# Soft-capped attention followed by mixture-of-experts attention on one core: joined score fills, gates and slot sums on GpSimd, and a different order of the work

## The chip, the cores and the metric

The kernel runs on one core of a Trainium2 chip. The metric is device microseconds (us) of one execution; the kernel before took a median of 336.59 us over 3 runs (334.86 to 338.03). The engines are TensorE (PE, with its weight loads as PEld), VectorE (DVE), ScalarE (ACT), GpSimd (POOL) and SyncE (SP, which here only issues transfers). Each runs its own instructions in the order in which they were written, and waits on semaphores for the others.

## What is computed

Two stages. The first is attention with a soft cap over 8 batches, 12 heads, 448 positions and a head width of 64; the second is a mixture of four attention experts on its output.

```python
# stage 1, for each of B=8 batches and H=12 heads; S=448, Dh=64, cap=30
scores = cap * tanh((q @ k.T / sqrt(64)) / cap)
attn = softmax(scores)                   # over the keys
x = attn @ v                             # heads side by side: 8 x 448 x 768
# stage 2, E=4 experts, the two best of each position
logits = x @ w_gate                      # 768 -> 4
topk = the two largest logits;  w = softmax over these two
for e in range(4):
    a = softmax(causal(x @ wq[e] @ (x @ wk[e]).T / sqrt(64)))
    ye = a @ (x @ wv[e]) @ wo[e]         # 64 -> 768
    out += (e in topk) * w_of_e * ye     # 8 x 448 x 768, float32
```

## The kernel before

**Pairs and batches.** The first stage goes by pairs of heads: 6 pairs in each of 8 batches, 48 in all (`NP`, with `HP` = 6). In a matmul a pair takes the two halves of the 128 rows, 64 for each head. One pair is made up as follows, with the lines of the code in brackets.

- SP issues loads of q, k and v (float32) for two pairs at a time. The last 64 of the 448 keys, the tail, are loaded apart. GpSimd casts all of it to float16 (k L485, q L488, k tails `ktz` L493, v L497, v tails `vtz` L504); of pairs 0 and 1, VectorE casts k, q and the k tails.
- PE transposes q and k (L513, L523) into one PSUM bank, and VectorE copies it to the tile `qk` (L544; L534 for pair 0).
- PE makes the scores (function `fill`). X is a PSUM tile of 3 banks, Y one of 2. X takes key block 0 of both heads, as two matmuls over 64 rows each (L555), and the tail keys of both heads, as one matmul over all 128 rows (L564, called sT). Y takes key block 1 (Y1), and once it has been read, key block 2 (Y2); each is two 64-row matmuls at L555. A matmul over 64 of the rows is called half-row below, one over all of them full-row.
- ACT takes the tanh of X, Y1 and Y2 (L577) into the tile `yp`, and then one exp over the 7 x 448 columns of the pair (L587). In order of time ACT does, for each pair, tanh X, tanh Y1, the exp of the pair before, tanh Y2.
- PE multiplies by v (L600 tails, L607), with a column of ones beside v that gives the row sums. VectorE divides (L627, L629). PE transposes the result (L641), and VectorE copies it to `xT` (L649), which is x of the batch, transposed.

**The gate stage.** When the 6 pairs of a batch are done, the second stage of this batch is mixed into the pairs of the next one. It works with two slots, one for the best expert of a position and one for the second best.

- PE computes v of all experts and the four logits (L662); VectorE copies the logits to `lg` and the values to `vB` (L671, L674). PE computes q and k of the experts (L686).
- The gate: VectorE compares all pairs of logits of a position (`g_c`, `g_d`, L711 to L715), sums the comparisons to a rank (L717), makes a mask for each slot by comparing with the tiles `rank0` and `rank1` (`ms`, L720), and finds the difference of the two best logits with two maxima (L722 to L726). ACT takes one small exp of it (`gexp`, L731). VectorE turns that into the weights `mw` (L739 to L745).
- GpSimd spreads the masks over 64 columns (`mB`, L753), PE transposes them (L763), and VectorE multiplies q with them (`qm`, L771). So the scores of a slot are those of the chosen expert.
- PE makes the scores of a slot in the banks of X (L792), ACT takes the exp (L801), GpSimd cuts the causal triangle. PE multiplies by `vB` (L850) and VectorE divides and weights (`oB`, one for each slot, L863 and L865).
- PE transposes the sum of the two slots: L880 multiplies both with the identity and accumulates, 16 matmuls in a batch. VectorE copies to `oT` (L888), PE multiplies by wo (L903), VectorE copies to `ob` (L912), and SP stores it.

The gate stage of batch 7 has no pairs beside it. Function `last` does it with more parallel work (L945, L954, L966, L987 to L1094).

**The order.** The order on each engine comes from a planner in the kernel's own Python (`Graph`). Each step is an `Op` with an engine, a duration `occ`, a time `lat` after which its result can be used, and what it reads and writes. ACT's main steps (tanh, exps) are a fixed chain that sets due times (`dues`); `solve` then walks in time, and takes for each engine the ready step with the earliest due time, by these numbers. Steps whose name is in `first` (fills, transposes of q and k, their casts and copies) go ahead of others. Steps that need a PSUM bank take one of A0 to A2; some may also borrow banks of X when they would give it back in time. The planner works with estimated durations, and the program it leaves is fixed.

**The start.** Seven matmuls of zeros (L1122) run on PE before the first data come. Loads of the expert weights (L455) and memsets (L393, for instance) stand on GpSimd's queue among the first casts.

## Time and profile before

| | before |
|---|---|
| median of 3 runs | 336.59 us |
| the profiled execution: its own time | 336.45 us |
| its span | 334.4 us |
| PE busy | 293.5 us (88%), 3435 instructions |
| ACT busy | 291.7 us (87%), 232 instructions |
| DVE busy | 239.2 us (72%), 752 instructions |
| POOL busy | 160.6 us (48%), 451 instructions |
| mean granted clock of TensorE | 0.99 |

The span is the time from the first to the last instruction of the profiled execution; its own time includes what lies around that. In rows that begin with a time, the columns are the start in us, the duration in us (of all, where several follow each other and a count such as x4 stands at the end), the engine, the line, the operation, what it writes <- what it reads, and in brackets the idle time just before it and what ended that. In rows of waits the columns are the line that waits <- the line that released it, then the sum in us, the number of waits, and the longest. In rows that begin with a line, the sum in us and the mean in ns stand behind the first bar, the engine's idle time before them behind the second.

### The profile page before, as it was taken

What the parts mean: (1) busy time and instruction counts of PE and PEld (TensorE: products, weight loads), DVE (VectorE), ACT (ScalarE), POOL (GpSimd) and SP (SyncE); (2) the same over time, 40 slices, a digit from 0 to 9 for tenths busy, and PEclk for the clock granted to TensorE, in tenths of its full rate; (3) what the DMA queues carried; (4) which work ended last, traced back from release to release, by engine and by line L of the source; (5) the groups of instructions that cost most, each with busy time, mean ns of one, the idle gap of its engine ahead of it and who ended that gap; (6) DMA issues with size and microseconds to landing.
All of it is one profiled execution on the core that took longest, in us unless ns stands there. A gap on an engine that the chain in (4) does not pass through costs nothing.

```text
span 334.4 us, 8992 instructions
## 1 busy us (share of the span) xinstructions
PE 293.5 (88%) x3435; PEld 193.5 (58%) x3435; DVE 239.2 (72%) x752; ACT 291.7 (87%) x232; POOL 160.6 (48%) x451
## 2 busy tenths in 40 slices
PE   6777779998998989998999899998998899978873
PEld 2244456475656756575666756675656666655542
DVE  5133536876859788877898778877896788756683
ACT  2699999989999899999989999999998999699152
POOL 8689889866216752376243941476243501110030
PEclk9998989999999999999999999999999999999999
DMA  9999999978923647338624845430211002200224
GB/s 162 228 262 236 254 237 224 254 173 229 266 91 126 193 114 234 102 85 226 156 105 119 225 129 186 128 104 2 98 47 25 3 15 81 74 0 2 96 71 167
DMA packets 65291, 46.21 MB, mean 138 GB/s; under 512 B 25888, under 2 KB 61856, under 8 KB 65248
## 3 DMA queue, kind: packets, MB, share of 16 engines
q1 hardware_dynamic: 54032, 43.30, 47.9%
q0 software_dynamic: 10512, 1.58, 7.2%
q10 hardware_dynamic: 704, 0.75, 0.8%
q8 instruction: 27, 0.44, 0.6%
q14 instruction: 16, 0.13, 0.1%
HBM read 36.19 MB, written 11.01 MB: 141 GB/s over the span
## 4 chain that ended last, share of the span: by engine, by line
PE 56%; DVE 17%; POOL 7%; DMA 6%; issue 5%; ACT 5%; SPq 1%; ACTq 0%; DVEq 0%; POOLq 0%
PE A L607 7%; PE A L686 7%; PE A L662 6%; PE Y L555 5%; PE A L903 5%; PE A L600 4%; DVE oB L865 3%; PE A L641 3%; DMA ktf<-in_k_dram 3%; PE X L792 3%; PE X L564 3%; PE A L850 2%; ACT yp L577 2%; PE X L555 2%; DVE oT L888 2%
## 5 line engine op out<-in xcount | busy, mean ns | idle before, releaser
L587 ACT ACTIVATE yp<-yp 128x3136 f16<-128x3136 f16 (+2 forms) x49 | 135.7, 2772 | 0.0
L577 ACT ACTIVATE yp<-Y 128x896 f16<-128x896 f32 x96 | 88.8, 925 | 10.0 <-PE Y L555 9.2
L577 ACT ACTIVATE yp<-X 128x1344 f16<-128x1344 f32 x48 | 62.5, 1302 | 3.7 <-PE X L555 2.2
L607 PE MATMUL A<-v,yp 128*128 128x65 f16 x1152 | 58.1, 197 | 0.0
L607 PEld LDWEIGHTS <-yp 128*128 128x128 f16 x1152 | 51.7, 100 | 4.6 <-issue 3.0
L497 POOL CAST v<-vf 128x384 f16<-128x384 f32 x48 | 24.5, 509 | 54.4 <-issue 36.2
L600 PE MATMUL A<-vtz,yp 128*128 128x130 f16 x192 | 43.2, 226 | 6.6 <-ACT yp L587 3.0
L629 DVE TENSOR_TENSOR xk<-A,rca 128x256 f16<-128x256 f32 x96 | 40.5, 423 | 2.7
L485 POOL CAST k<-kf 128x384 f16<-128x384 f32 x46 | 23.3, 506 | 30.8 <-PE A L523 18.9
L544 DVE COPY qk<-A 128x960 f16<-128x960 f16 x47 | 29.6, 650 | 11.7 <-PE A L513 11.4
L627 DVE RECIPROCAL rca<-A 128x4 f32<-128x4 f32 x96 | 16.9, 177 | 28.0 <-PE A L607 27.6
L555 PE MATMUL Y<-qk 64*128 64x448 f16 x192 | 36.2, 373 | 0.7 <-ACT yp L577 0.5
L912 DVE COPY ob<-A 128x384 f32<-128x384 f32 (+1 forms) x55 | 29.3, 552 | 3.2 <-PE A L903 2.4
L488 POOL CAST q<-qf 112x512 f16<-112x512 f32 x46 | 28.3, 615 | 2.8 <-DMA qf<-in_q_dram 1.6
L903 PE MATMUL A<-wo,oT 128*128 128x384 f16 x114 | 26.6, 328 | 1.8 <-DVE oT L888 1.3
L600 PEld LDWEIGHTS <-yp 128*128 128x128 f16 x192 | 18.9, 99 | 15.2 <-issue 9.3
L753 POOL CAST mB<-ms 128x1024 f16<-128x1024 f32 x14 | 14.2, 1041 | 27.2 <-DVE ms L720 25.8
L555 PEld LDWEIGHTS <-qk 64*128 64x128 f16 x288 | 14.2, 93 | 22.0 <-issue 16.9
L523 PE MATMUL A<-ident,k 128*128 128x128 f16 x144 | 16.9, 229 | 10.5 <-POOL k L485 7.1
L504 POOL CAST vtz<-vtf 64x64 f16<-64x64 f32 x96 | 22.7, 236 | 3.1
L513 PE MATMUL A<-ident,q 112*128 112x112 f16 x192 | 23.1, 223 | 1.2 <-POOL q L488 1.2
L493 POOL CAST ktz<-ktf 64x64 f16<-64x64 f32 x92 | 21.6, 235 | 3.6 <-DMA ktf<-in_k_dram 0.3
(140 smaller groups left out, 569.2 us busy)
## 6 DMA issues: line engine op xcount, KB each, us to landing
qf<-in_q_dram SPq DMA_DIRECT2D x23, 448.0 KB, 6.4
kf<-in_k_dram SPq DMA_DIRECT2D x23, 384.0 KB, 5.3
vf<-in_v_dram SPq DMA_DIRECT2D x23, 384.0 KB, 5.1
out_dram<-ob SPq DMA_DIRECT2D x23, 384.0 KB, 2.9
out_dram<-ob SPq DMA_DIRECT2D x8, 192.0 KB, 2.7
ktf<-in_k_dram SPq DMA_DIRECT2D x46, 32.0 KB, 5.0
vtf<-in_v_dram SPq DMA_DIRECT2D x46, 32.0 KB, 4.7
qf<-in_q_dram ACTq DMA_DIRECT2D x2, 224.0 KB, 4.0
```

What stands on the lines that cost most here:

```text
L488: put(0.4, 0.56, lambda e: e.tensor_copy(q16[i], qf[s][:, h].rearrange("p h (c d) -> p c h d", c=QC)), [("qf", x)], [("q16", i)], head, f" ...
L497: nc.gpsimd.tensor_copy(v16[u][:, :, :, 0:Dh], vf[s][:, h].rearrange("p h (c d) -> p h c d", c=KC))
L544: lambda: nc.vector.tensor_copy(qk[t], bank16(g)[:, 0 : S + 512]),
L555: nc.tensor.matmul(dst[:, g, 0:S], qk[t][r, S + 128 * (c + 1) : S + 128 * (c + 2)], qk[t][r, 0:S], start=True, stop=True,)
L577: ACTS[what, p] = act(c_act(S * (b - a)), lambda: nc.scalar.activation(y[:, a:b, :], src[:, 0 : b - a, 0:S], AF.Tanh, scale=isc / capf), [ ...
L587: act(c_act(S * (b - a), False), lambda a=a, b=b: nc.scalar.activation(y[:, a:b, :], y[:, a:b, :], AF.Exp, scale=capf), ks, ks, fixed=True ...
L600: nc.tensor.matmul(ps[:, n, :, :], y[:, 2, w : w + 128], vtz[u], start=(n == 0), stop=False, skip_group_check=True,)
L607: nc.tensor.matmul(ps[:, n, h, :], y[:, SLOT[c][h], w : w + 128], v16[u][:, h, c, :], start=False, stop=(c == 2), skip_group_check=True,)
L629: dve(c_dve(256), lambda g=g, i=i, rc=rc: nc.vector.tensor_tensor(xk[p % NXK][:, 2 * i : 2 * i + 2, :, :], view(g)[:, :, :, 0:Dh], rc.broa ...
L686: pe(S, lambda g=g, w2=w2, j=j: nc.tensor.matmul(bank(g)[:, 0:S], w2[:, j, :], xT[x][:, j, :], start=(j == 0), stop=(j == NDC - 1)), [("xT ...
L903: nc.tensor.matmul(bank(g)[:, 0 : D // 2], oT[x][r][:, w : w + 128], wo2[r][:, c0:c1], start=(r == 0), stop=(r == 1),)
L912: e(o[lo:128, c0:c1], bank(g)[lo:128, 0 : D // 2])
```

## The change

It has five parts.

1. **Joined fills.** `fill` makes the Y2 scores of a pair and the X scores of the next pair one step of four half-row matmuls, where no gate-stage score stands between them (33 of 47 places). Counted from 0, the two slots of a batch are scored beside pairs 5 and 6 after it where it was 4 and 5 (`XOFF`), those of batch 6 beside 4 and 5 where it was 3 and 4.
2. **The gate on GpSimd.** All of it before the small exp, and the weights `mw` after it, are GpSimd operations. The form is another one: a signed difference, sums by halves (`g_h`, `g_k`) and constants in place of the rank tiles. Two operations after the exp stay on VectorE.
3. **Slot sums on GpSimd.** Two GpSimd additions make `oS`, the sum of the slots, in float16; PE transposes it with 8 transposes in a batch where 16 accumulating matmuls stood.
4. **The start.** Zero matmuls: 9 of 512 columns, then 30 of 128 columns wherever PE has nothing else (`NWARM`, `NFILL`). Pair 0's k cast is ACT's, the q casts of pairs 0 to 3 are VectorE's, all k tails are GpSimd's. Casts and transposes of each pair are written one pair earlier. The expert weights' loads are due 12 us later.
5. **The planner's numbers.** A change between half-row and full-row work costs 0.1 (`SWITCH`); PE takes twice as long before 5.5 us (`WARM`); transfers share a wire (`LAND`, `RATE`); due times follow the lag of ACT's chain; one solve stands where three did, each of which started from the times of the one before.

```diff
+SWITCH = 0.1
+WARM = 5.5
+LAND = 2.9
+NWARM = 9
+NFILL = 30
+RATE = 230.0
...
+            if e == "PE" and o.half != half:
+                t = max(t, free.get(e, 0.0) + SWITCH)
...
-                    d = u.due if u.first else max(u.due, t0 + 0.8)
-                    return d - (u.grp is not None and not u.opens), u.due, u.idx
+                    d = u.due + lag if u.first else max(u.due + lag, t0 + 0.8)
+                    d -= u.grp is not None and not u.opens
+                    return d - 2.0 * (u.half and half), u.due, u.idx
...
+        if p == 0:
+            act(c_act(KM, False), lambda: kc(nc.scalar.copy), *kio, name=f"k16_{p}", fixed=True)
+        else:
+            gp(0.45, lambda: kc(nc.gpsimd.tensor_copy), *kio, name=f"k16_{p}")
+        if p < 4:
+            dve(0.48, lambda: qc(nc.vector.tensor_copy), *qio, name=f"q16_{p}", lat=0.56)
+        else:
+            gp(0.56, lambda: qc(nc.gpsimd.tensor_copy), *qio, name=f"q16_{p}")
...
+        if what == "X" and p and p - 1 not in exps:
+            pass
+        elif what == "Y2" and p < NP - 1 and p not in exps:
+            pe(0, lambda: (heads(p, "Y2"), heads(p + 1, "X")), rd(p) + rd(p + 1),
+               both + [("s", XB[0]), ("s", XB[1])], occ=0.385, name=f"sY2X_{p}",
+               takes=YB + XB[0:2])
+        else:
+            pe(0, lambda: heads(p, what), rd(p), both, occ=0.195, name=f"s{what}_{p}",
+               takes=bs[0:2])
...
-        V = nc.vector
+        V = nc.gpsimd
...
+        g_(lambda: V.tensor_tensor(g_c[x], lb(), la(), ALU.subtract), L, ["c"], 0.22)
+        g_(lambda: V.tensor_scalar(g_d[x], g_c[x], 0.0, None, ALU.is_equal), [(b, "c")], ["d"],
+           0.2)
...
+        for i in range(2):
+            n = slice(2 * i, 2 * i + 2)
+            gp(1.1, lambda n=n: nc.gpsimd.tensor_tensor(oS[:, n], oB[0][:, n], oB[1][:, n], ALU.add),
+               [("oB", s, m) for s in range(2) for m in (2 * i, 2 * i + 1)], [("oS", i)],
+               name=f"oS{b}")
...
+                for n in range(4):
+                    nc.tensor.transpose(
+                        bank16(g)[:, 128 * n : 128 * (n + 1)],
+                        oS[:, n, 2 * r : 2 * r + 2, :].rearrange("p e d -> p (e d)"),
+                        ident if n < 3 else swap,
+                    )
...
-    XOFF = (4, 5)
...
+    XOFF = (5, 6)
+    exps = {HP * (b + 1) + (XOFF if b < LB - 1 else (4, 5))[s]: (b, s) for b in range(LB) for s in range(2)}
...
+    for i in range(NWARM + NFILL):
+        n = 512 if i < NWARM else 128
...
-    for _ in range(3):
-        G.dues(when)
-        order = G.solve(AUX, XB + YB)
-        when = {o.idx: o.start for o in fixed}
+    G.dues(when)
+    order = G.solve(when, AUX, XB + YB)
```

Some rows of the order show it at three places. The names end in the number of a buffer; lines are those of the kernel that the rows come from, so that a fill is L555 before and L580 now, and sT is L564 before and L601 now.

On PE, at the second Y fill of pair 3, before (`qk3` is the q and k of pair 3, `qk0` here that of pair 4, and `xk1` is a finished result that is being transposed; the two half-row matmuls that fill X from `qk0` stand ahead of its four transposes, the last of which is the first row):

```order
L641 MATMUL A1_66<-pswap_183,xk1_125 128x128
L564 LDWEIGHTS qk0_116
L564 MATMUL X_63<-qk0_116 128x448
L555 LDWEIGHTS qk3_119
L555 MATMUL Y_64<-qk3_119 128x448
L555 LDWEIGHTS qk3_119
L555 MATMUL Y_64<-qk3_119 128x448
L523 LDWEIGHTS k16_0_91
```

And now, at the same fill:

```order
L601 LDWEIGHTS qk0_116
L601 MATMUL X_63<-qk0_116 128x448
L580 LDWEIGHTS qk3_119
L580 MATMUL Y_64<-qk3_119 128x448
L580 LDWEIGHTS qk3_119
L580 MATMUL Y_64<-qk3_119 128x448
L580 LDWEIGHTS qk0_116
L580 MATMUL X_63<-qk0_116 128x448
L580 LDWEIGHTS qk0_116
L580 MATMUL X_63<-qk0_116 128x448
L681 LDWEIGHTS xk1_125
```

The half-row matmuls of X, which stood ahead of the transposes of `xk1` and of sT, now stand directly behind those of Y; of the four changes between half-row and full-row work, two are left.

The start: on VectorE before, the casts of pairs 0 and 1 (`q16`, `k16`, and the tails `ktz`) and the copy to `qk0`:

```order
L488 CAST q16_0_88<-qf0_68 112x512
L485 CAST k16_0_91<-kf0_72 128x384
L493 CAST ktz0_94<-ktf0_80 64x64
L488 CAST q16_1_89<-qf0_68 112x512
L493 CAST ktz0_94<-ktf0_80 64x64
L485 CAST k16_1_92<-kf0_72 128x384
L534 COPY qk0_116<-A1_66 128x576
L493 CAST ktz1_95<-ktf0_80 64x64 x2
```

On GpSimd now, behind the memsets, with `wvg` the weights for v and the gate:

```order
L419 MEMSET ktz5_99 128x128
L476 DMA wvg_181<-in_moe_w_gate_dram 128x6x4
L476 DMA wvg_181<-in_moe_wv_dram 128x6x64
L515 CAST ktz0_94<-ktf0_80 64x64
L476 DMA wvg_181<-in_moe_wv_dram 128x6x64
L515 CAST ktz0_94<-ktf0_80 64x64
L476 DMA wvg_181<-in_moe_wv_dram 128x6x64
L498 CAST k16_1_92<-kf0_72 128x384
L515 CAST ktz1_95<-ktf0_80 64x64 x2
```

The tails of pairs 0 and 1 went from VectorE to GpSimd, where issues of the weights' loads stand ahead of them and between them.

The gate of batch 1: on VectorE before, its first operations (`lg1` the logits, `qB1` and `kB1` the experts' q and k):

```order
L671 COPY lg1_137<-A2_67 128x4
L674 CAST vB1_135<-A2_67 64x4x64
L712 TENSOR_TENSOR g_d1_192<-lg1_137 128x64
L711 TENSOR_TENSOR g_c1_190<-lg1_137 128x64
L713 TENSOR_TENSOR g_d1_192<-g_d1_192,tri_186 128x64
L722 TENSOR_REDUCE g_m11_198<-lg1_137 128x4
L715 TENSOR_TENSOR g_c1_190<-g_c1_190,g_d1_192 128x64
L694 CAST qB1_1_141<-A1_66 128x448
L649 COPY xT0_132<-A0_65 128x448
L627 RECIPROCAL rca2_130<-A2_67 128x4
L717 TENSOR_REDUCE g_r1_194<-g_c1_190 128x16
```

On GpSimd now, from the slot sums of the batch before:

```order
L929 TENSOR_TENSOR oS_158<-oB0_156,oB1_157 128x512 x2
L753 TENSOR_TENSOR g_c1_189<-lg1_137 128x64
L754 TENSOR_SCALAR g_d1_191<-g_c1_189 128x64
L756 TENSOR_SCALAR g_c1_189<-g_c1_189 128x64
L757 TENSOR_TENSOR g_d1_191<-g_d1_191,tri_187 128x64
L758 TENSOR_TENSOR g_c1_189<-g_c1_189,g_d1_191 128x64
L760 TENSOR_TENSOR g_h1_197<-g_c1_189 128x32
L762 TENSOR_TENSOR g_r1_193<-g_h1_197 128x16
L766 TENSOR_SCALAR ms01_205<-g_r1_193 128x16
L766 TENSOR_SCALAR ms11_207<-g_r1_193 128x16
L807 CAST mB0_146<-ms01_205 128x1024
L807 CAST mB1_147<-ms11_207 128x1024
```

The gate left VectorE's queue, where copies of other steps stood between its operations, and stands on GpSimd's in one piece, with both mask casts right behind it and ahead of the four operations that give the small exp its input.

## What was predicted before the kernel ran

> **What bounds the kernel now.** I read the page first, for the span and the busy shares.
>
> ```profile
> span 334.4 us, 8992 instructions
> PE 293.5 (88%) x3435; PEld 193.5 (58%) x3435; DVE 239.2 (72%) x752; ACT 291.7 (87%) x232; POOL 160.6 (48%) x451
> ```
>
> Two engines are close to full: TensorE (PE) at 88% and ScalarE (ACT) at 87%. VectorE (DVE) has a quarter free and GpSimd (POOL) half. The profiled execution took 336.45 us, so 2.05 us lie outside its span; the median of the runs, 336.59, is 0.14 above it, and I count from 336.45. Next, ACT in order of time: the first work, one pair in the steady state, and the end of the softmax stream.
>
> ```profile
> 8.52 0.92 ACT L577 ACTIVATE yp<-Y 128x896 f16<-128x896 f32 x1 [1.75 <-PE Y L555]
> 12.07 1.29 ACT L577 ACTIVATE yp<-X 128x1344 f16<-128x1344 f32 x1 [0.59 <-PE X L564]
> 15.36 0.92 ACT L577 ACTIVATE yp<-Y 128x896 f16<-128x896 f32 x1 [2.00 <-PE Y L555]
> 21.80 0.92 ACT L577 ACTIVATE yp<-Y 128x896 f16<-128x896 f32 x1 [0.83 <-PE Y L555]
> ...
> 25.32 0.91 ACT L577 ACTIVATE yp<-Y 128x896 f16<-128x896 f32 x1
> 26.12 1.29 ACT L577 ACTIVATE yp<-X 128x1344 f16<-128x1344 f32 x1
> 27.29 0.93 ACT L577 ACTIVATE yp<-Y 128x896 f16<-128x896 f32 x1
> 28.09 2.84 ACT L587 ACTIVATE yp<-yp 128x3136 f16<-128x3136 f16 x1
> 30.79 0.94 ACT L577 ACTIVATE yp<-Y 128x896 f16<-128x896 f32 x1
> ...
> 299.11 1.03 ACT L801 ACTIVATE pB<-X 128x1024 f16<-128x1024 f32 x1
> ...
> 306.29 2.96 ACT L587 ACTIVATE yp<-yp 128x2240 f16<-128x2240 f16 x2
> ```
>
> One pair is tanh Y (second half of the pair before), tanh X, tanh Y, exp: from 25.32 to 30.79, 5.47 us when nothing waits. Forty-eight of them are 262.6; the 14 gate-stage exps (L801, 1.03 less the 0.12 by which the next instruction overlaps) are 12.7 more, and 7 small ones about 1: 276. The stream runs from 8.52 to 309.25 (306.29 + 2.96), 300.7 us. So the span is 8.5 of head, 276 of ACT work that the change leaves alone, about 24 in which ACT waits, and 25.15 of tail (309.25 to 334.4). What ACT waits for is the third view, its waits by releaser:
>
> ```profile
> ACT yp L577 <- PE Y L555: 9.2, 16, 2.0
> ACT g_e L731 <- DVE g_e L726: 4.2, 6, 1.3
> ACT yp L577 <- PE X L555: 2.2, 4, 0.8
> ACT pB L801 <- PE X L792: 1.6, 1, 1.6
> ACT yp L577 <- DVE qm L771: 0.8, 1, 0.8
> ```
>
> Score fills (L555, L564) and gate-stage scores hold ACT for 13.8 us in these rows (9.2 + 2.2 + 1.6 + 0.8), about 15.5 with the smaller ones, the small exp of the gates for 4.2. Of the fills' part, 5.2 us are in the head: 1.75 before the first tanh, then 0.59, 2.00 and 0.83 in the rows above. The remaining 10.3 are spread over pairs 3 to 47. A wait also loses the 0.12 us by which two ACT instructions otherwise overlap (25.32 + 0.92 against 26.12), which is how 18 listed become 24. Why fills come late is seen on PE; its first two rows are windows (length, then busy time of PE, PE's weight loads, DVE, ACT and POOL, then clock, DMA share and rate):
>
> ```profile
> 20.00:60.00 40.00, 31.89 (x366) 20.33 (x365) 19.20 (x57) 38.60 (x28) 35.76 (x121) 0.91 1.23 242
> 22.00:300.00 278.00, 253.99 (x3065) 170.88 (x3062) 209.68 (x656) 263.11 (x199) 140.17 (x393) 0.99 0.54 139
> ...
> 14.04 0.29 PE L523 MATMUL A<-ident,ktz 128*128 128x128 f16 x1 [0.89 <-POOL ktz L493]
> 14.76 0.56 PE L555 MATMUL Y<-qk 64*128 64x448 f16 x2
> 28.00 0.36 PE L555 MATMUL X<-qk 64*128 64x448 f16 x2
> 28.29 0.34 PE L641 MATMUL A<-perm,xk 128*128 128x128 f16 x3
> 28.52 0.35 PE L564 MATMUL X<-qk 128*128 128x448 f16 x1
> 28.81 0.36 PE L555 MATMUL Y<-qk 64*128 64x448 f16 x2
> 30.90 0.41 PE L523 MATMUL A<-ident,k 128*128 128x128 f16 x3 [1.73 <-POOL k L485]
> ...
> 305.83 0.50 PE L880 MATMUL A<-ident,oB 128*128 128x128 f16 x8
> 306.56 0.92 PE L945 MATMUL X<-xT,wk 128*128 128x448 f16 x4
> ```
>
> In the middle PE is busy 254.0 of 278 us, so a fill usually stands behind other work in PE's queue. A 448-column matmul with all rows takes a place of 0.19 us ((0.92 - 0.35) / 3 at 306.56). The two half-row matmuls of the fill at 28.00 run side by side, and yet the next full-row work begins 0.29 later; in front of the fill at 28.81 the same 0.10 is lost again (28.52 + 0.19 = 28.71). Each change between half-row and full-row work costs about 0.10. The clock is the second thing: the same fill takes 0.56 at 14.76 and 0.36 at 28.00, and the transposes at 30.90, after 1.73 us without work, are slow again (0.41 for three, 0.34 at 28.29).
>
> **The change part by part.** *Joined fills.* 33 of the 47 second-Y fills now also fill X of the next pair (all but those where a gate-stage score uses X between). Each join drops two row changes: 33 x 2 x 0.10 = 6.6 us of PE. The wait it cannot touch is that of the first Y fill, which still stands alone: it may start only when the tanh before has freed Y, and must be done within the tanh of X, 1.17 us later; the waits at 15.36 and 21.80 are of this kind. X is now filled while the exp runs, so X banks are lent less: of the gate stage's groups 4 mask transposes and 7 value products lay in X, now 1 and 0. A group that finds no bank makes PE wait for a DVE copy.
>
> *Slot sums.* Per batch 16 matmuls that added two slots become 8 transposes. The eight at 305.83 took 0.50, about 0.045 apart, so 7 x 8 x 0.045 = 2.5 us of PE go, and the two DVE copies read f16. With the joins PE loses 9.1 us of work. PE is in front of ACT in about half of those places (16 + 4 fill waits beside 48 first-Y fills), so I take half, -4.5; the bounds are 0 (the fills wait as before) and -9.1.
>
> *GpSimd.* Every batch POOL gets two slot sums, 13 gate operations before the small exp and 3 after it. No two-input operation runs on POOL in this trace. The nearest rows:
>
> ```profile
> L753 POOL CAST mB<-ms 128x1024 f16<-128x1024 f32 x14 | 14.2, 1041 | 27.2 <-DVE ms L720 25.8
> L488 POOL CAST q<-qf 112x512 f16<-112x512 f32 x46 | 28.3, 615 | 2.8 <-DMA qf<-in_q_dram 1.6
> L504 POOL CAST vtz<-vtf 64x64 f16<-64x64 f32 x96 | 22.7, 236 | 3.1
> ...
> 62.78 1.01 DVE L741 TENSOR_SCALAR g_w<-g_e 128x4 f32<-128x4 f32 x1
> ```
>
> A slot sum has 512 outputs and 1024 inputs: between 0.615 (512 elements cast) and 1.041 (1024 cast). I take 1.04, since both inputs must be read. A gate operation of 16 to 64 elements lies near the 64-element cast, 0.236; the row at 62.78 gives the other end: a 4-element DVE operation took 1.01 us beside the mask cast on POOL, so operations of these two engines can hold each other up. I take 0.25, and 0.24 to 0.55 for the range. The Trainium skill ("GPSIMD Engine Reference", 3.1 Elementwise — side-by-side cycle accounting) gives 2.6 cycles an element for two inputs; that would make a slot sum an estimated 1.1 us of elements before its overhead, so 0.1 to 0.2 per batch more, and no row here shows it. The chain from the last oB to the small exp becomes 2 x 1.04 + 13 x 0.25 + 2 mask casts of 1.04 = 7.4 us, all of it in POOL's queue in front of casts for later pairs; but those are issued one pair earlier than before, and POOL's 160.6 us grow only by 8 x 16 x 0.25 + 7 x 2.08 = 47. ACT does not see the length of the chain, only how late it is against the place in ACT's queue where the planner put the small exp. The planner's own costs in the diff add up to 2.28 + 2 x 1.1 + 2 x 1.1 = 6.7, 0.7 under mine. ACT instructions being 0.8 to 2.8 long, the planner leaves a chance slack of up to one of them, so I take no change in the 4.2 us, with -3.5 and +8 as ends. DVE loses the gate operations, which shortens what stands before qk copies and kB; that is worth something only through PE, and is in the half above.
>
> *Head.* Pair 0's k cast moves to ACT, its tail casts (L493, now L515) from DVE to POOL, behind the memsets and two weight DMAs, with a third between the two casts:
>
> ```profile
> 1.32 0.21 POOL L393 MEMSET ktz<- 128x128 f16 x1
> 2.36 0.97 POOL L455 DMA_DIRECT2D wvg<-in_moe_w_gate_dram  x1
> 3.33 2.48 POOL L455 DMA_DIRECT2D wvg<-in_moe_wv_dram  x3
> ```
>
> A block of memsets takes 1.04 (1.32 to 2.36). Three of them and one more end at 4.6; the two DMAs at 0.97 and 0.83 (2.48 / 3) at 6.4; cast, DMA, cast (0.3, 0.83, 0.3) at 7.85. The transpose of the tails then takes PE to 8.0, seven zero matmuls follow, and only then the first Y fill. With a fast clock that is 8.0 + 0.4 + 0.36 = 8.8, with a slow one 8.1 + 0.75 + 0.56 = 9.4. So the first tanh is later than 8.52, by 0.3 (to 0.9). What comes behind gains more. In before PE stood still ahead of 14.04 (0.89) for POOL's casts of pair 2, which cost ACT the 2.00 at 15.36; now the k transposes of pairs 2 and 3 stand in front of that fill, cast by about 11.6 (7.85, then a k cast, two tails, memsets, a DMA and two k casts: 0.5 + 0.6 + 0.8 + 0.83 + 1.0), and their q and tails behind it, under the exp. Without a wait the first Y tanh of pair 2 comes at 8.8 + 4 x 0.8 + 3 x 1.17 + 2.7 = 18.2; I take 18.5 in place of 21.80 (-3.3). The one of pair 3 stands behind transposes of pair 5, whose tails, counted in the same way through three more weight DMAs, leave POOL at about 24.2, where ACT wants the fill done by 23.9: with transpose and fill +1.1. Sum -2.2, between -3.5 and +1.
>
> The clock in this stretch is a choice. Slow rows follow idle time (14.76, and 30.90 after 1.73), fast ones follow dense work (28.00). The 39 zero matmuls (9 of 512 columns, 30 of 128) where 7 stood keep PE at work up to the first transposes, so I take fast; slow throughout makes it -1.5. The Trainium skill ("TensorE: Matmul & The Clock Gate", Part 1: The HAM clock gate) says that about 3.4 us of sustained work release the full clock and an idle stretch as long takes it back. The trace agrees with the first half, as the zero matmuls of before end short of that:
>
> ```profile
> 1.26 3.17 PE L1122 MATMUL A<-warm 128*128 128x512 f16 x7 [1.26 <-DVE warm L387]
> ```
>
> It does not agree with the second: 1.73 us were enough. By the page the head is -2.2.
>
> *Tail.* The last gate-stage score moves one pair later, so all eight L912 copies of batch 6 now come behind the stream; in before the third of them stood at 310.32.
>
> ```profile
> L912 DVE COPY ob<-A 128x384 f32<-128x384 f32 (+1 forms) x55 | 29.3, 552 | 3.2 <-PE A L903 2.4
> L713 DVE TENSOR_TENSOR g_d<-g_d,tri 128x64 f32<-128x64 f32 x8 | 1.7, 219 | 0.0
> 310.32 0.54 DVE L912 COPY ob<-A 128x384 f32<-128x384 f32 x1
> ```
>
> Three more at 0.55 less overlap are +1.4 on DVE, ten gate operations less (the row at 219 ns is one of them) about -2. The values (L966, 18 matmuls) move ahead of the last transpose, about -1; the gates on POOL start behind a slot sum, up to +1 on the exps. I take -0.5, ends -2 and +2.
>
> **Sum.** 336.45 - 2.2 - 4.5 + 0 - 0.5 = 329.2 us, 2.2% below.
>
> **Rivals.** *A: GpSimd late.* If a gate operation takes 0.55 in place of 0.25, the chain is 3.9 longer; less a mean slack of 0.9, ACT waits 3 us in each of 7 batches where it waited 0.6: +17, giving 329.2 + 17 = 346. It decides from about 0.40 an operation, where the 7.2 us of the sum are used up. For: the row at 62.78. Against: POOL's own small casts, at a mean of 0.236 over 96. The Trainium skill ("GPSIMD Engine Reference", 4.1 Engine selection) advises VectorE for two-input elementwise work; no row here tests it. *B: nothing comes through.* The first-Y fills wait as before, since each is bound by one tanh of X, and the head's gain goes into POOL's queue, which is busy 35.8 of 40 us up to 60: 336.45 - 0.5 = 336. For: the long Y waits at 15.36 and 21.80 are first-Y fills. Against: PE's rows have no idle time in front of them. *C: PE was the whole cause.* All 9.1 come through, the planner's truer costs take the small exp's wait to 1, and the tail gains 2: 336.45 - 3.5 - 9.1 - 3.2 - 2 = 318.7. *D: fewer banks.* PE waits 0.2 us for a bank at about 40 groups, +8 on the forecast: 337; for it, the X rows of these groups; against, there were 11 of them in over 100.
>
> **Chances.** Forecast (324 to 333) 0.42, C 0.21, B 0.19, A 0.12, D 0.06. A per cent is about what a measurement of this kernel tells from no change: faster is below 333.1, slower above 339.8. Faster: 0.42 less 0.02, C 0.21, a tenth of B: 0.62. Slower: A 0.12 and half of D with a little of B: 0.17. Same: 0.21. The range leaves out the lower half of C and the upper half of A: 318 to 340.
>
> **What would show it.** ACT's wait for Y falls from 9.2 to under 5 and that for X under 2; its wait for g_e, now released by POOL, stays near 4; first tanh at 8.6 to 9.4; Y tanh of pair 2 before 20; POOL slot sums near 1.1 and gate operations near 0.25; stream end to span end near 24.6. I am wrong if the g_e wait passes 10, or if Y waits stay at 9 while PE's row changes fall.

## The result, and the profile after

The changed kernel took a median of 325.30 us over 4 runs (324.38 to 325.98), the kernel before 336.51 us over 4 (334.86 to 338.03): a ratio of 0.9666, with a 95% interval of 0.9612 to 0.972. So 11.2 us went. The forecast was 329.2 within 318 to 340. The profiled execution took 325.84 us. These are three rows of its page; the last is the granted clock in 40 slices of the span, in tenths:

```profile
span 324.1 us, 8923 instructions
PE 286.5 (88%) x3411; PEld 190.2 (59%) x3411; DVE 215.9 (67%) x636; ACT 289.8 (89%) x233; POOL 207.4 (64%) x595
...
PEclk9987989999999999999999999999999999999997
```

ACT is still near full and GpSimd went from 160.6 to 207.4 us, VectorE from 239.2 to 215.9. The span is 10.3 shorter, 334.4 to 324.1. ACT's waits by releaser, with the columns as before (sum, number, longest):

```profile
ACT yp L617 <- PE Y L580: 3.8, 5, 2.4
ACT pB L855 <- PE X L846: 3.2, 3, 2.1
ACT g_e L787 <- POOL g_e L782: 2.3, 4, 0.8
ACT yp L617 <- PE X L580: 1.0, 2, 0.5
```

The waits for Y fills fell from 9.2 to 3.8, and 2.42 of that stand before the first tanh; the wait for the small exp fell from 4.2 to 2.3; that for the first scores of a batch (`pB`, L855) rose from 1.6 to 3.2. ACT in order of time, from the head; the two long exps that bound the middle of the stream (31.71 and 289.40), between them two gate-stage scores one pair apart; then its end:

```profile
8.63 0.92 ACT L617 ACTIVATE yp<-Y 128x896 f16<-128x896 f32 x1 [2.42 <-PE Y L580]
19.04 0.92 ACT L617 ACTIVATE yp<-Y 128x896 f16<-128x896 f32 x1 [0.40 <-PE Y L580]
...
31.71 2.81 ACT L627 ACTIVATE yp<-yp 128x3136 f16<-128x3136 f16 x1
...
73.83 1.06 ACT L855 ACTIVATE pB<-X 128x1024 f16<-128x1024 f32 x1
...
80.21 1.10 ACT L855 ACTIVATE pB<-X 128x1024 f16<-128x1024 f32 x1
...
289.40 2.84 ACT L627 ACTIVATE yp<-yp 128x3136 f16<-128x3136 f16 x1
...
293.81 2.95 ACT L627 ACTIVATE yp<-yp 128x2240 f16<-128x2240 f16 x2
```

The same two exps of the kernel before, those of pairs 3 and 46 counted from 0:

```profile
33.97 2.81 ACT L587 ACTIVATE yp<-yp 128x3136 f16<-128x3136 f16 x1
...
302.78 2.86 ACT L587 ACTIVATE yp<-yp 128x3136 f16<-128x3136 f16 x1
```

I use these two exps in every run below, as they divide the span in three.

- **Head**, up to the exp of pair 3: 33.97 before, 31.71 now, -2.3.
- **Middle**, between the exps of pairs 3 and 46: 268.8 before, 257.7 now. In both kernels a pair in which nothing waits takes 5.47 us, a gate-stage score 0.91 more (6.38 in all, from 73.83 to 80.21), a small exp 0.10 more. There are 43 pairs, 7 small exps, and 14 scores before but 13 now, since one moved behind pair 46. What is left is what ACT lost: 268.81 - 235.21 - 12.74 - 0.70 = **20.2** before, 257.69 - 235.21 - 11.83 - 0.70 = **9.95** now, -10.2.
- **End**, from the exp of pair 46 on: 31.6 before (6.5 to the end of the stream and 25.15 of tail), 34.7 now (7.4 and 27.34). Of the +3.1, 0.9 is the score that moved, and +2.2 is the tail.

-2.3, -10.2 and +2.2 make up the 10.3. (The score's 0.9 only changed sides.) The 20.2 can be split by the kind of pair in which they fell: pairs with neither score nor small exp 7.7, with scores 5.7, with a small exp 6.7. After, the same are 0.9, 5.9 and 3.2.

All these figures come from one traced execution of each kernel. How far they can be trusted is seen in runs below that leave a stage alone. Two that change only zero matmuls ahead of it or behind it lost 9.6 and 9.75 us in the middle, and two with the tail as it is had 27.40 and 27.43 there; but in two with the head as it is the exp of pair 3 began at 32.3 and 32.6. So I read differences of a microsecond in the middle or the tail, and none under a microsecond in the head.

### The profile page after: what moved, and what is told of

Same layout as the page of the kernel before. It is cut to its first block, busy times and chain, and to the rows that moved or that the text cites. A ratio compares the mean times of both kernels' runs of the same rounds, so it can differ in the third digit from the quotient of the medians.

```text
span 324.1 us, 8923 instructions
## 1 busy us (share of the span) xinstructions
PE 286.5 (88%) x3411; PEld 190.2 (59%) x3411; DVE 215.9 (67%) x636; ACT 289.8 (89%) x233; POOL 207.4 (64%) x595
## 4 chain that ended last, share of the span: by engine, by line
ACT 45%; PE 23%; POOL 17%; DVE 7%; issue 4%; DMA 3%; SPq 0%; ACTq 0%; POOLq 0%; DVEq 0%
ACT yp L617 21%; ACT yp L627 19%; ACT pB L855 3%; PE A L647 3%; PE Y L580 2%; PE A L702 2%; PE A L726 2%; PE A L960 2%; POOL mB L807 2%; POOL v L519 2%; POOL ktz L515 2%; DVE ob L969 2%; POOL k L498 2%; DMA vf<-in_v_dram 2%; PE X L846 1%
## 5 line engine op out<-in xcount | busy, mean ns | idle before, releaser
L627 ACT ACTIVATE yp<-yp 128x3136 f16<-128x3136 f16 (+2 forms) x49 | 137.7, 2813 | 0.0
L617 ACT ACTIVATE yp<-Y 128x896 f16<-128x896 f32 x96 | 92.0, 958 | 4.0 <-PE Y L580 3.8
L617 ACT ACTIVATE yp<-X 128x1344 f16<-128x1344 f32 x48 | 64.2, 1337 | 1.1 <-PE X L580 1.0
L647 PE MATMUL A<-v,yp 128*128 128x65 f16 x1152 | 56.2, 196 | 0.0
L580 PE MATMUL Y<-qk 64*128 64x448 f16 x192 | 35.7, 366 | 4.3 <-ACT yp L617 2.6
L969 DVE COPY ob<-A 128x384 f32<-128x384 f32 (+1 forms) x57 | 30.8, 553 | 5.2 <-PE A L960 4.6
L960 PE MATMUL A<-wo,oT 128*128 128x384 f16 x118 | 28.3, 339 | 1.0 <-DVE oT L1152 0.2
L919 DVE SCALAR_TENSOR_TENSOR oB<-A,rcb,mw 128x256 f16<-128x256 f32 x56 | 26.1, 482 | 2.5 <-POOL k L498 0.5
L501 POOL CAST q<-qf 112x512 f16<-112x512 f32 x44 | 26.9, 614 | 0.7
L580 PEld LDWEIGHTS <-qk 64*128 64x128 f16 x288 | 14.1, 93 | 22.4 <-issue 14.8
L929 POOL TENSOR_TENSOR oS<-oB,oB 128x512 f16<-128x512 f16 x14 | 16.1, 1153 | 14.0 <-DVE oB L919 6.6
L535 PE MATMUL A<-ident,q 112*128 112x112 f16 x192 | 21.8, 214 | 2.1 <-POOL q L501 2.1
```

What stands on the lines that cost most here:

```text
L580: nc.tensor.matmul(dst[:, g, 0:S], qk[t][r, S + 128 * (c + 1) : S + 128 * (c + 2)], qk[t][r, 0:S], start=True, stop=True,)
L617: ACTS[what, p] = act(c_act(S * (b - a)), lambda: nc.scalar.activation(y[:, a:b, :], src[:, 0 : b - a, 0:S], AF.Tanh, scale=isc / capf), [ ...
L627: act(c_act(S * (b - a), False), lambda a=a, b=b: nc.scalar.activation(y[:, a:b, :], y[:, a:b, :], AF.Exp, scale=capf), ks, ks, fixed=True ...
L647: nc.tensor.matmul(ps[:, n, h, :], y[:, SLOT[c][h], w : w + 128], v16[u][:, h, c, :], start=False, stop=(c == 2), skip_group_check=True,)
L960: nc.tensor.matmul(bank(g)[:, 0 : D // 2], oT[x][r][:, w : w + 128], wo2[r][:, c0:c1], start=(r == 0), stop=(r == 1),)
L969: e(o[lo:128, c0:c1], bank(g)[lo:128, 0 : D // 2])
```

## The experiments

### Each part undone alone

Three runs put one part of the change back, and leave the others and the planner as they are.

The first writes the two fills as two steps again:

```diff
-        if what == "X" and p and p - 1 not in exps:
+        if False:
             pass
-        elif what == "Y2" and p < NP - 1 and p not in exps:
+        elif False:
```

> The changed kernel, with the second-Y fill and the next X fill written as two steps again. If PE's load is what made the fills late (the theory), 33 x 2 row changes x 0.10 = 6.6 us of PE come back, and as in the prediction about half of it reaches ACT: its waits for Y and X fills behind pair 3 rise from about 1 us to 3 to 5, and the time from 325.3 to 328 or 329. If the planner's truer numbers and the earlier casts had done it (the rival), ACT's waits for fills stay near 1 and the time within 1 us of 325.3.

It took 330.7 us (ratio to before 0.9822, 0.9788 to 0.9856): 5.4 more than the changed kernel, and more than half of 6.6. ACT's exps of pairs 3 and 46, and its largest wait:

```profile
30.61 2.87 ACT L627 ACTIVATE yp<-yp 128x3136 f16<-128x3136 f16 x1
...
294.16 2.84 ACT L627 ACTIVATE yp<-yp 128x3136 f16<-128x3136 f16 x1
```

```profile
ACT pB L855 <- PE X L846: 9.7, 6, 2.4
```

Middle: 263.55 - 247.74 = 15.8 lost (247.74 is 235.21 + 11.83 + 0.70), 5.9 more than with the joins. How much work PE got back can be counted in its rows: 242 changes between half-row and full-row work in the middle, where the changed kernel has 194 (in the whole run 274, where it has 218 and the kernel before 284). These are 48, 4.8 us at 0.10, and PE is busy 4.9 us longer in the middle (244.35 against 239.43). So all of it reached ACT, and about 1 us more, not half. But it came back in another place than I expected. The plain pairs lost 1.1, as little as with the joins; the first score of a batch is what waits, 9.7 us in place of 3.2. The head and the tail of the traced execution are shorter (by 1.1 and 0.75), so that its span is 4.0 longer and not 5.9.

The second has the gate and the weights on VectorE, in the form of before:

```diff
-        V = nc.gpsimd
+        V = nc.vector
...
-            gp(occ, fn, r, [(b, y) for y in w], lat=occ + 0.06, name=f"g{b}")
+            dve(occ, fn, r, [(b, y) for y in w], lat=lat, name=f"g{b}")
```

> The changed kernel, with the gate and the weights in the old form on VectorE. ACT's wait for the small exp's input and what it loses around it are 3.5 us less in the changed kernel than before. If the move to GpSimd did that, it comes back: time 328 to 329, the L-line of the small exp waiting 4 us. If it was where the planner put the small exp in ACT's queue, the time stays within 1 us of 325.3, or falls, since GpSimd's chain becomes 3.3 us shorter.

It took 327.54 us (0.9729, 0.9685 to 0.9772), 2.2 more, with intervals that overlap; that is neither the 328 to 329 of the first expectation nor within 1 us of 325.3. The exps:

```profile
32.03 2.84 ACT L635 ACTIVATE yp<-yp 128x3136 f16<-128x3136 f16 x1
...
289.51 2.84 ACT L635 ACTIVATE yp<-yp 128x3136 f16<-128x3136 f16 x1
```

Middle: 257.48 - 247.74 = 9.7, no more than 9.95: the small exps lost 1.2 more, the scores 1.0 less. So in the stream it made no difference which of the two engines has the gate; the tail was 0.9 longer. The rest of the 2.2 is within the spread of the runs.

The third has the 16 accumulating matmuls back:

```diff
-                    nc.tensor.transpose(
-                        bank16(g)[:, 128 * n : 128 * (n + 1)],
-                        oS[:, n, 2 * r : 2 * r + 2, :].rearrange("p e d -> p (e d)"),
+                        for s in range(2):
+                            nc.tensor.matmul(
+                                bank(g)[:, 128 * n : 128 * n + 128 - a],
+                                oB[s][:, n, 2 * r : 2 * r + 2, :].rearrange("p e d -> p (e d)"),
+                                ident[:, a:128], start=(s == 0), stop=(s == 1),
```

> The changed kernel, with the slot sums as 16 accumulating matmuls a batch again. PE gets 2.5 us more. By the theory that half of PE's load reaches ACT: 326.0 to 326.6, with the fill waits up by about 1. If PE has enough room since the joins, no change, 325.3; if GpSimd's slot sums held its queue, faster than 325.

It took 329.41 us (0.9805, 0.9757 to 0.9853), 4.1 more, beyond all three expectations.

```profile
31.61 2.84 ACT L627 ACTIVATE yp<-yp 128x3136 f16<-128x3136 f16 x1
...
291.38 2.84 ACT L627 ACTIVATE yp<-yp 128x3136 f16<-128x3136 f16 x1
```

Middle: 259.77 - 247.74 = 12.0, 2.1 more than now. Six of the seven batches have their sums in the middle, 6 x 8 x 0.045 = 2.2 us of PE work by the prediction's count, though PE's busy time grew by 1.1 only (240.50 against 239.43). The edit is not one of PE alone: it also turns 14 copies of VectorE from float16 to float32 (0.62 us each in place of 0.38) and takes the additions from GpSimd. More work on VectorE is not likely the cause, as the gate put 17 us on it in the middle (201.92 against 184.72) and ACT lost nothing by it; but this run does not separate the three. The tail grew as well, from 27.3 to 29.0.

### The three undone together, and the planner alone

All three edits in one kernel; the planner, the start, the earlier casts and the later scores stay:

```diff
-        if what == "X" and p and p - 1 not in exps:
+        if False:
...
-        V = nc.gpsimd
+        V = nc.vector
...
+                                ident[:, a:128], start=(s == 0), stop=(s == 1),
```

> The changed kernel without joins, gates and slot sums on GpSimd: what is left is the planner, the start and the earlier casts. If the three costs measured one by one (5.4, 2.2 and 4.1 us) add up, 325.3 + 11.7 = 337.0, no better than before: then these three are the whole gain. If they overlap (each alone makes PE or VectorE late at the same first score of a batch), 331 to 334, and the rest of the gain belongs to the planner and the start.

335.76 us (0.9974, 0.9951 to 0.9996): 10.5 more than the changed kernel, where the three add up to 11.7. So they hardly overlap, and what remains of the change is worth about one us by itself.

```profile
30.79 2.87 ACT L635 ACTIVATE yp<-yp 128x3136 f16<-128x3136 f16 x1
...
296.54 2.84 ACT L635 ACTIVATE yp<-yp 128x3136 f16<-128x3136 f16 x1
```

```profile
ACT pB L849 <- PE X L840: 15.1, 6, 4.2
```

Middle: 265.75 - 247.74 = 18.0. The small exps, whose input VectorE makes here, lost nothing at all (the view of waits has no row for them), and nearly everything, 15.1, stands at the scores.

Then the kernel before, with the new planner and nothing else:

```diff
+SWITCH = 0.1
...
+            if e == "PE" and o.half != half:
+                t = max(t, free.get(e, 0.0) + SWITCH)
...
-    for _ in range(3):
-        G.dues(when)
-        order = G.solve(AUX, XB + YB)
-        when = {o.idx: o.start for o in fixed}
+    G.dues(when)
+    order = G.solve(when, AUX, XB + YB)
```

> The kernel before with the new planner alone: its costs of row changes, slow start and transfers, the lag term, one solve; no fill, gate, sum or cast is changed. In the run without joins the plain pairs lost 1.1 us where before lost 7.7, and the joins were not the reason. If the planner's numbers moved the waits away for good, 7.7 + 6.7 (plain and gate pairs) fall to about 2 + 4 and the time is 328 to 331. If PE's work is the bound and the planner only chooses where it shows, the waits turn up at the first score of each batch and the time stays at 335 to 337.

335.43 us (0.9947, 0.9918 to 0.9977).

```profile
31.69 2.87 ACT L614 ACTIVATE yp<-yp 128x3136 f16<-128x3136 f16 x1
...
300.51 2.88 ACT L614 ACTIVATE yp<-yp 128x3136 f16<-128x3136 f16 x1
```

```profile
ACT pB L828 <- PE X L819: 10.5, 5, 4.4
```

This run has 14 scores between the two exps, as before: 268.82 - 248.65 = 20.2, the very loss of before. Only the places changed: plain pairs 1.6, scores 11.2, small exps 7.5. The head is 2.3 shorter and the tail 2.0 longer. The second expectation held: the planner chose where PE's backlog shows.

That it is PE's backlog is seen best in PE's busy time between the two exps. In these rows stand the stretch, its length, then the busy time of PE, of its weight loads, of DVE, ACT and POOL, and the clock third from the end; they are the kernel before, the planner alone, the three undone, and the changed kernel:

```profile
33.97:302.78 268.81, 247.64 (x2986) 166.92 (x2985) 207.19 (x649) 254.17 (x194) 130.00 (x364) 0.99 0.50 134
...
31.69:300.51 268.82, 250.32 (x2985) 169.17 (x2984) 206.11 (x648) 251.56 (x194) 127.96 (x363) 0.98 0.51 136
...
30.79:296.54 265.75, 247.27 (x2966) 164.52 (x2965) 201.53 (x640) 250.02 (x194) 128.75 (x359) 0.99 0.51 138
...
31.71:289.40 257.69, 239.43 (x2924) 161.39 (x2922) 184.72 (x543) 250.71 (x193) 169.15 (x479) 0.99 0.52 142
```

With the new planner the length of the middle is PE's busy time and 18.5, 18.5 and 18.3 us more (19.2 without the joins, 19.3 without the slot sums, 17.9 with the gate on VectorE); in the kernel before it is 21.2 more. The three parts took 7.8 us of PE's busy time away, and ACT lost 8.1 less. The granted clock is 0.98 or 0.99 in all of them, and 0.99 both with the three undone and in the changed kernel, so it is not what makes this difference.

### The work without the planner

```diff
-    G.dues(when)
-    order = G.solve(when, AUX, XB + YB)
+    for _ in range(3):
+        G.dues(when)
+        order = G.solve(AUX, XB + YB)
+        when = {o.idx: o.start for o in fixed}
```

> The changed kernel with all its work where it is, but ordered by the planner of before (no cost of row changes, three solves). If the work is what counts, 325 to 327. If the join needs the planner (the join alone in before gave nothing), 331 to 336, with the waits at fills back above 5 us.

This kernel has every part of the change, ordered by `solve` as it was before. It took 338.93 us (1.0066, 1.004 to 1.0092): slower than before, and 13.6 slower than the changed kernel.

```profile
37.37 2.81 ACT L609 ACTIVATE yp<-yp 128x3136 f16<-128x3136 f16 x1
...
300.95 2.84 ACT L609 ACTIVATE yp<-yp 128x3136 f16<-128x3136 f16 x1
```

```profile
ACT yp L599 <- PE Y L562: 8.5, 12, 2.0
ACT g_e L769 <- POOL g_e L764: 6.7, 6, 2.4
```

Middle: 263.58 - 247.74 = 15.8. So in the middle the whole change brought 4.3 us with the old planner and 10.2 with the new one. Head (37.37 against 33.97) and tail (29.1 against 25.15) gave back 3.4 and 4.0. PE has as few row changes in the middle as in the changed kernel (198, there 194), and yet is busy 245.05 us for the same work, 5.6 more; why is not known.

The join alone, in the kernel before and with its planner:

```diff
+        elif what == "Y2" and p < NP - 1 and p not in exps:
+            pe(0, lambda: (heads(p, "Y2"), heads(p + 1, "X")), rd(p) + rd(p + 1),
```

> The kernel before, with the joined fills alone (and casts and transposes written a pair earlier, which the join needs), its planner and its numbers as they were. By the theory half of 6.6 us: 336.5 - 3.3 = 333.2. By the rival, that the planner's numbers are needed, 336 or slower.

336.38 us (0.9992, 0.9965 to 1.0019), no change.

```profile
35.97 2.81 ACT L598 ACTIVATE yp<-yp 128x3136 f16<-128x3136 f16 x1
...
302.47 2.88 ACT L598 ACTIVATE yp<-yp 128x3136 f16<-128x3136 f16 x1
```

Middle, with 14 scores: 266.50 - 248.65 = 17.9, 2.3 less than before; the head gave back 2.0 and the tail 1.1. PE's busy time in the middle fell by 5.6 us (242.06 against 247.64), so that the old planner left more than half of what the join saved as idle time of PE.

### The places of the scores

```diff
-    exps = {HP * (b + 1) + (XOFF if b < LB - 1 else (4, 5))[s]: (b, s) for b in range(LB) for s in range(2)}
+    exps = {HP * (b + 1) + (XOFF if b < LB - 1 else (3, 4))[s]: (b, s) for b in range(LB) for s in range(2)}
```

> The changed kernel with the scores of batch 6 beside pairs 3 and 4 again. The tail behind the last stream exp grew from 25.15 to 27.34 us. If the later score is the reason (more of batch 6's wo and copies behind the stream), the tail falls by 1 to 2 us and the time to 323.3 to 324.3. If the reason is the slow clock of the last wo matmuls behind a 1.6 us gap on PE, the tail stays within 0.5 of 27.3 and the time at 325.

330.61 us (0.9798, 0.9754 to 0.9843), 5.3 more: both expectations failed. ACT's waits for the scores of a batch:

```profile
ACT pB L855 <- PE X L846: 5.3, 4, 3.3
```

The longest of them, 3.3 us where it is 2.1 now, is for the first score of batch 6, and the tail did not shrink but grew to 29.4 (299.53, the end of the stream, to 328.9). Of the 4.8 us by which the span is longer, 0.9 are in the head, 1.9 are more loss of ACT in the middle, and 2.0 are tail.

```diff
-    XOFF = (5, 6)
+    XOFF = (6, 7)
```

> The changed kernel with the scores of batches 0 to 5 one pair later again (beside pairs 6 and 7); batch 6 stays. In every run with the new planner ACT's largest waits stand at the first score of a batch (5.9 of 9.95 us in the changed kernel). If that score is simply due too early, one pair of 5.5 us more lets PE catch up: of the waits at the first scores of batches 1 to 5 (3.5 us) at most 0.5 is left, and the time falls to about 322. If PE's work over a whole batch is the bound and the planner only chooses where it shows, the same 9 to 11 us turn up at the small exps or the fills, and the time stays at 325.3 within 1.

379.08 us (1.1233, 1.1169 to 1.1297), 54 more; neither expectation held. ACT in order of time, in one of the batches, and its largest wait:

```profile
234.40 0.20 ACT L787 ACTIVATE g_e<-g_e 128x4 f32<-128x4 f32 x1 [7.82 <-POOL g_e L782]
234.52 1.01 ACT L855 ACTIVATE pB<-X 128x1024 f16<-128x1024 f32 x1
```

```profile
ACT g_e L787 <- POOL g_e L782: 46.4, 6, 13.0
```

PE began the values of the next batch (L702) here:

```profile
224.39 2.85 PE L702 MATMUL A<-wvg,xT 128*128 128x260 f16 x24
```

The small exp of this batch now stands in ACT's queue right ahead of a score exp of the batch before, and ACT waits for the whole gate from 224.39 on, a chain that otherwise runs beside other work of ACT. It did so in six waits of 46.4 us together. So one pair later is too late: the gate stages of two batches collide, which neither theory had thought of, and the question between them stays open.

### The clock

Three runs change only zero matmuls. The first puts twelve into the largest gap of PE in the tail:

```diff
+        pe(0, zero, ["warm", ("pvL", 2), ("pvL", 3)], ["tailzero"], gz, occ=0.11 * 12, name="zero")
```

> The changed kernel with twelve zero matmuls of 256 columns on PE in the tail, between the last value products and the last transposes, where PE stood idle for 1.60 us; nothing else. If that gap made the clock fall (the theory), the granted clock in the last 8 us stays at 1.0, the ten wo matmuls behind it take 0.17 to 0.2 us apiece instead of 0.36, and the time falls by 1 to 2 us, to 323.3 to 324.3. If the tail is bound by copies and stores whatever the clock, 325.3 within 0.5.

PE in the tail of the changed kernel, behind the gap:

```profile
314.20 0.34 PE L1144 MATMUL A<-ident,oB 128*128 128x128 f16 x3 [1.60 <-DVE oB L1136]
...
315.94 1.78 PE L960 MATMUL A<-wo,oT 128*128 128x384 f16 x5 [0.25 <-DVE oT L1152]
```

And with zero matmuls in it:

```profile
312.81 1.47 PE L1143 MATMUL X<-warm 128*128 128x256 f16 x12
...
316.54 0.99 PE L960 MATMUL A<-wo,oT 128*128 128x384 f16 x5 [0.25 <-DVE oT L1159]
```

In stretches of 3 us behind the same point of the stream (the clock is the third number from the end), the changed kernel, and then the run with zeros:

```profile
314.76:317.76 3.00, 2.45 (x11) 1.21 (x12) 1.49 (x4) 0.48 (x1) 0.00 (x0) 0.66 0.10 21
317.76:320.76 3.00, 2.35 (x10) 1.01 (x8) 1.68 (x3) 1.22 (x3) 0.00 (x0) 0.77 0.69 265
```

```profile
314.99:317.99 3.00, 2.29 (x18) 1.25 (x16) 2.28 (x6) 0.58 (x2) 0.00 (x0) 1.00 0.09 19
317.99:320.99 3.00, 1.16 (x8) 0.49 (x5) 1.25 (x3) 1.33 (x3) 0.00 (x0) 1.00 0.81 309
```

Five wo matmuls took 0.99 us in place of 1.78, at a granted clock of 1.00 in place of 0.66 over the stretch. The theory of the clock holds for PE. The time does not follow: 325.53 us (0.9643, 0.9609 to 0.9678), no change. ACT's last copy begins 22.56 us behind the end of the stream, in place of 23.74, and yet the span ends only 0.33 sooner. The clock was not what ended the tail; what does end it, behind the last issue of a store, has no row in these views.

The second puts zeros into gaps of the head:

```diff
+        nz = 16 if 2 <= p <= 7 else 0
...
+            for _ in range(nz):
+                nc.tensor.matmul(bank(g)[:, 480:512], warm[:, 0:128], warm[:, 0:32], start=True,
...
+                    nz = 8 if 2 <= p <= 6 and i == 0 and n == 0 else 0
```

> The changed kernel with zero matmuls in front of the tail transposes of pairs 2 to 7 and in front of the value products of pairs 2 to 6, where PE stood idle for 2.12 and 1.83 us and the clock was 0.66 and 0.62 in the stretch behind. If the clock holds the head up, it stays near 1.0 up to 50 us, the exp of pair 3 starts at 30.5 rather than 31.7, and the time falls by about 1 us to 324.3. If GpSimd's casts are what the head waits for, no change, or up to 1 us slower for the added PE work.

326.78 us (0.9699, 0.9648 to 0.9751), 1.5 more. The clock was 1.00 from 28 to 48 us (0.57 from 16 to 20, 0.70 from 24 to 28) and the exp of pair 3 started at 31.66 as now (31.71).

The third takes zeros away:

```diff
-NWARM = 9
-NFILL = 30
+NWARM = 7
+NFILL = 0
```

> The changed kernel with the seven zero matmuls of before where it has nine long and thirty short ones. The prediction took 1.5 us as the price of a slow clock in the head. If the zero matmuls are worth it, the first fills take 0.56 and the first tanh starts at 9.2 or later (8.63 now), and the time is 326 to 327. If the clock falls soon afterwards anyway (it was 0.66 at 16 to 20 us with them), 325.3 within 0.7.

325.34 us (0.9643, 0.9606 to 0.968): no change. From 8 to 12 us the clock was 0.63 in place of 1.00; in stretches of 4 us, this run, and then the changed kernel:

```profile
8.00:12.00 4.00, 3.63 (x26) 1.62 (x22) 1.14 (x3) 3.61 (x4) 3.63 (x12) 0.63 1.77 233
```

```profile
8.00:12.00 4.00, 3.11 (x28) 1.39 (x26) 1.24 (x3) 3.37 (x4) 3.63 (x12) 1.00 1.70 241
...
16.00:20.00 4.00, 3.65 (x38) 2.12 (x36) 1.85 (x5) 3.38 (x5) 3.60 (x10) 0.66 1.55 232
```

The first Y fill took 0.56 us, as expected, where it takes 0.36 now; but it began at 7.65 in place of 8.22, since no zero matmuls stood ahead of it. So the first tanh was even earlier, 8.24 in place of 8.63, and the exp of pair 3 at 31.43. In all three rows GpSimd is busy 3.6 of 4 us, so that its casts are the likelier bound of the head; that was not tried.

## Why the prediction was right or wrong

**What bounds the kernel: right.** ACT's waits were the reserve, and they are set by PE's work. The runs say it more sharply than the prediction did: with one planner, PE work put back shows up in ACT's loss about us for us (4.9 us of PE's busy time and 5.9 of loss for the joins, 7.8 and 8.1 for all three parts).

**Joined fills and slot sums: right in kind, the size wrong.** "PE is in front of ACT in about half of those places (16 + 4 fill waits beside 48 first-Y fills), so I take half, -4.5" is the term that was mis-sized. The count behind it was right: the changed kernel has 66 row changes fewer (218 against 284). The middle lost 10.2 us less; the three parts account for 8.1 of it (18.0 - 9.95), and 2.1 came with the rest of the change (20.2 - 18.0), but not with the planner alone. Counting the places where a fill was late says how the old order spread the backlog, not how much backlog there is: the new planner alone took 6 us of loss out of the plain pairs, and the same loss stood at the scores. Rival C, that PE was the whole cause, had this term nearly right (-9.1); its 318.7 is 7 us too low because it took 3.2 off the small exps on top, 2 off the tail, which grew by 2.2, and 3.5 off the head in place of 2.3. That the fills' waits would fall was right; that "the wait it cannot touch is that of the first Y fill" was wrong: between the exps of pairs 3 and 46 the waits for Y fills were 4.6 us before, 1.0 with the planner alone, and 0.2 now.

**The planner.** I gave its numbers no term, except in rival C. They have one, and not by themselves: beside the runs of before that go with them, planner alone -1.4 (336.8 to 335.4), work alone +2.1 (to 338.9), both -11.2. With the old planner the prediction's half came true in the middle (4.3 of 9.1), and head and tail took it back. Which of its numbers does it, the cost of a row change, the lag or the single solve, was not tried.

**GpSimd: right.** The operations in the changed kernel, by groups (sum, mean in ns):

```profile
L929 POOL TENSOR_TENSOR oS<-oB,oB 128x512 f16<-128x512 f16 x14 | 16.1, 1153 | 14.0 <-DVE oB L919 6.6 <-PE A L681 5.1 <-DVE rcb L917 2.0
L754 POOL TENSOR_SCALAR g_d<-g_c 128x64 f32<-128x64 f32 x8 | 3.1, 382 | 0.7
L758 POOL TENSOR_TENSOR g_c<-g_c,g_d 128x64 f32<-128x64 f32 x8 | 2.6, 320 | 0.5
L782 POOL TENSOR_TENSOR g_e<-g_k 128x4 f32<-128x4 f32 x8 | 1.6, 202 | 0.6
```

A slot sum took 1.15 us where I took 1.04. The 2.6 cycles an element of the Trainium skill ("GPSIMD Engine Reference", 3.1 Elementwise — side-by-side cycle accounting), an estimated 1.1 us and an overhead, were closer. A gate operation took 0.20 to 0.38, about 0.27 in the mean of the thirteen operations of a batch, where I took 0.25. Rival A fell; it needed 0.40 by my figure, and 0.44 by the working that gave its +17, as the 0.40 leaves out the 4.2 that ACT waited already. The change of 0 for the gate's place was right in the stream (9.7 against 9.95). The small exps' loss did fall, from 6.7 to 3.2, but not by GpSimd: with all three parts undone, and so with the gate on VectorE, it was 0. I take it as one more place where PE's backlog showed.

**Head: the sum right, its reasons not.** -2.2 was forecast, -2.3 measured; the first tanh came at 8.63 (forecast 8.6 to 9.4), that of pair 2's first Y at 19.04 (forecast 18.5). But the planner alone, with the old start and casts where they were, has the exp of pair 3 at 31.69, and the whole new start under the old planner at 37.37. So the head's gain came from the order, and not from where a cast stands, on which my working rested; that the sum agreed is luck. The fast clock on which I also rested is there for the first fills (0.36 at 8.22, where the first fill of before took 0.56 at 7.92) and gone by the fill at 15.90 (0.56); the run with seven zero matmuls shows that it is not needed. My reading that slow rows follow idle time does not fit the row at 14.76: in before every fill from 7.92 to 23.61 took 0.55 to 0.60, those ahead of the idle 0.89 too.

**Tail: wrong, even in sign.** I took -0.5 with ends of -2 and +2; it was +2.2. "Three more" copies behind the stream had no basis: in before the first copy of batch 6 began at 309.10, the stream ended at 309.25, and the row at 310.32 is already behind it. Nor is the later score the reason, as the run with the score moved back has a longer tail still, and the planner alone, which has that score at the old place, has 27.1. So an order alone can make 2.0 of the 2.2. The new planner is not needed for it either: every other order that was tried has a longer tail than that of before, with the old planner 26.25 (the join alone) and 29.1 (the whole change). In the changed kernel about 0.3 of it is the slow clock (27.34 with it, 27.01 without). The planner alone has that slow clock too (0.67, 0.50 and 0.69 in three stretches of 3 us from 322 to 331), where before had 1.00, and how much of its 2.0 this makes was not tried. The rest stays open.

**The sum.** -2.2 - 4.5 + 0 - 0.5 against -2.3 - 10.2 + 2.2: one term was less than half of what it should be, and one of a wrong sign took back part of that. The time lay within the range, and in the forecast's own part of it (324 to 333), the latter in part by luck: had the tail come out as I took it, -0.5, the time would have been 2.7 lower, about 323.

## What to carry to other kernels

Where one engine's waits are spread over many small places, add them up over the stage and compare the sum with the work of the engine that causes them; the label of a wait only says where the order lets the backlog appear, and an order that moves it was worth little here until the work shrank too. Where a planner writes the order, a change of the work and a change of the planner have to be tried in all four combinations, since here the planner alone gave 0.5%, the work alone cost 0.7%, and both together gave 3.3%. A slow clock on an engine is worth mending only where that engine is what ends the stretch.

## What the hardware showed that I had not expected

The granted clock fell in the last 8 us of the changed kernel, and the wo matmuls took 0.36 us apiece (1.78 / 5). It did not fall in the gap of 1.60 us: the transposes behind it, at 314.20, still took 0.34 for three, and the record shows 1.00 up to 315.6 and 0.50 from 315.8 on. Twelve zero matmuls in the gap, 1.47 us of work, held it at 1.00. The Trainium skill ("TensorE: Matmul & The Clock Gate", Part 1: The HAM clock gate) has the clock fall after an idle window of about 3.4 us. Here no such window was empty: in the 3.40 us from 312.60 to 316.00 PE was busy for 1.09, most of it transposes, and in the head of the kernel before, in the 3.40 us up to 31.10, where the record falls, for 1.64. So the prediction's "1.73 us were enough" names only the longest gap of a stretch in which PE was busy less than half the time.

The record of the granted clock has a blind spot at the start: in the kernel before it shows 1.00 from the first us to 30.9, while the fill at 14.76 took 0.56 us and that at 28.00 took 0.36. There the durations tell the clock, and the mean of 0.99 is too high.

A 4-element operation on GpSimd took 0.20 us and one of 64 elements 0.29 to 0.38, in a queue full of casts. The operation that makes the small exp's input took 0.55 us in the mean on VectorE before (0.16 to 0.85), and 0.20 on GpSimd now, in all eight batches:

```profile
L726 DVE TENSOR_TENSOR g_e<-g_m,g_m 128x4 f32<-128x4 f32 x8 | 4.4, 552 | 0.2
```
